# A Fourier mixer and a low-rank MLP on one core: first group of batch 0 closed by selection matmuls, loads held back, stage-2 loads issued at other steps

## The chip, the cores and the metric

The kernel runs on one core of a Trainium2 chip. The metric is the device time of one launch in microseconds (us). A core has a matrix engine (TensorE, PE in the profile; PEld are its weight loads), a vector engine (VectorE, DVE), a scalar engine (ScalarE, ACT), a general engine (GpSimd, POOL), and SyncE (SP), which here only issues transfers. Each engine works through its own list of instructions in order. DMAs are issued by SP, ACT and POOL, each in the order of its list; those that change the type on the way (f32 to f16) are issued by POOL. Matrix products end in PSUM (8 banks of 512 f32 a partition), and are brought to SBUF by ACT or DVE.

## The reference

For eight batches of 3136 tokens with 256 channels each, the reference filters along the tokens in the frequency domain, then applies a low-rank mixing along the tokens and a two-layer MLP along the channels, each with what it reads added:

```python
X = np.fft.rfft(x, axis=1)                                   # x: (8, 3136, 256)
y = np.fft.irfft(X * (filt_r + 1j * filt_i)[None], n=3136, axis=1)
u = y + (y.transpose(0, 2, 1) @ U @ V).transpose(0, 2, 1)    # U: (3136, 32), V: (32, 3136)
out = u + np.maximum(u @ w_ch1, 0.0) @ w_ch2                 # w_ch1: (256, 1024), w_ch2: (1024, 256)
```

## The kernel before

The transform of length 3136 is split as 64 x 49. For each batch there are four stages:

- Stage 1 (`st1`): the token axis of 64 points, by matmuls with the constant `wf`, for 49 residues in three tiles of 16 (`x[b, 0]` to `x[b, 2]`) and one last residue (`x[b, 3]`, tile `xl`). The result goes through DRAM (`ct1[b]`), since the next stage needs the residues on the partitions. `st1` is a generator of 13 pieces; each piece makes two matmuls of 256 columns and evicts one bank.
- Stage 2 (`two` in `plan_mid`, `stage2`): the residue axis, for eight "quads" of four frequencies; `load_a2` (`fetch`) brings one quad back from `ct1`. Then the product with the filter: `ta`, two halves of `tb`, and the sum `y` on POOL. The three products are made on DVE, or, for the quads in `on_pool`, on POOL after ACT has copied the bank (`pooled`). For this form the filter is rearranged in place into `fa` (= `fb`) and `fc`.
- Stage 3 (`three`, `stage3`, `out3`): back along the residues, two halves to a quad; ACT evicts to `esb`, SP stores a quad to DRAM (`ct2[b]`).
- Stage 4 (`stage4`): back along the 64 points, for groups of 512 tokens (`Group(b, c)`, c = 0 to 5; the last residues of two batches make one group of 128). `load_e2` fetches a group's tile `e` from `ct2` with the 64 frequency slots on partitions 0 to 63; `put_h` writes the low-rank part `h1` to partitions 64 to 95 of the same tile. So the matmul with `sv` adds the low-rank mixing as well. `low_rank` makes `h1` from all of `esb` and `uh`.

The MLP then runs over the groups. Each group has eight steps. A step makes two matmuls of the first layer (`mm1`, L488), one eviction with ReLU on ACT to the ring `hring` (L492), and one eighth of the second layer of the group before (`mm2_part`, L521, with the residual, L497). Steps 2 and 6 of a group also hold `stage4` of the next group. All other work of later batches is hung on steps by hand: `at(s, f, ...)` puts a call behind step s, `early[s]` ahead of it. There are 416 steps; `start[b]` is the first step of batch b; `later(s, n)` is n steps of full length after s.

Batch 0 is different, since nothing runs beside it. `turned` makes stage 1 with x as the stationary operand, and stores it in SBUF (`cm`, which lies in the space of `fc`); `mid_first` transposes it back on PE (`turn_a2`), and runs stage 2 and 3 with the filter as it was loaded: 16 halves `j`, a product `uv` with two results for each, and two matmuls with other constants in stage 3, so no sum is needed. For j = 7, 9, 12 and 14 POOL makes the product (L397), for the others DVE (L400). In `mid_first`, before these, POOL issues the loads of x of batch 1 and of the second weight `w2sb` (L384). After `mid_first` follow all of `st1(1)`, `low_rank(0)`, `put_h`, `stage4` of group 0, and the first half of `make_fa`; its second half is hung on steps 1 and 3. `keep_warm` are matmuls whose result is not used.

The plan of batch 1 begins five steps after the start of batch 0: stage 2 of its first quad at step 5, its last half of stage 3 at step 40, `load_e2(1, 0)` at step 41. Group 6, the first of batch 1, has its `stage4` on steps 46 and 47. For batch 2 stage 2 begins nine steps ahead of batch 1's first, and its first loads eight steps before that; stage 3 of batch 2 ends at 36 of the 50 steps of batch 1.

Of the kernel before, what the change touches and what calls it, by code (L numbers as in the profile page):

```python
# [14 lines left out]
SEQ = 3136  # L15
# [9 lines left out]
def _consts():  # L25
# [10 lines left out]
    wf = np.zeros((128, 25, 128))  # L36
    for h in range(2):
        wf[h::2, 0:24, 64 * h:64 * h + 64] = t1[:, 24 * h:24 * h + 24]
    wf[0:64, 24, 0:64] = t1[:, 48]
# [59 lines left out]
    return (wf.reshape(128, 25 * 128).astype(f16), w2.astype(f16), g3.astype(f16),  # L99
# [4 lines left out]
def kernel(  # L104
# [13 lines left out]
    names = ("wf", "w2", "g3", "s4", "su", "tw", "kr")  # L118
    wf_d, w2_d, g3_d, s4_d, su_d, tw_d, kr_d = (
# [22 lines left out]
    def bank(tag):  # L142
        of = {"m": (0, 1), "o": (2, 3), "w": (4,), "e": (7,), "f": (0, 1, 2, 3, 4, 7), "e0": (7, 4), "f0": (0, 1), "w1": (7, 5, 6)}[tag]
        turn[tag] = turn.get(tag, -1) + 1
        return psum[:, of[turn[tag] % len(of)], :]


    NH = 17
    hring = cst.tile([128, NH, 512], F16, name="hring")
# [3 lines left out]
    wf = cst.tile([128, 25, 128], F16, name="wf")  # L153
    for c in range(4):
        i = slice(8 * c, min(8 * c + 8, 25))
        nc.sync.dma_start(wf[:, i], wf_d.rearrange("p (i m) -> p i m", m=128)[:, i])
# [3 lines left out]
    def load_x(b, c, after=None):  # L160
        if c == 3:
            t = sb.tile([64, DM], F16, tag="xl", bufs=2, name="xl")
            nc.gpsimd.dma_start(t, dram(x.tensor, (b * SEQ + 48) * DM, [[NR * DM, 64], [1, DM]]))
        else:

            t = sb.tile([128, 4, XW], F16, tag="x", bufs=4, name="x")
            if after is not None:
                nc.gpsimd.tensor_copy(t[0:1, 0, 0:1], after[0:1, 0:1])
            for h in range(2):
                nc.gpsimd.dma_start(t[h:128:2, :, 0:2 * DM],  # L170
                                    dram(x.tensor, (b * SEQ + 24 * h + 8 * c) * DM,
                                         [[NR * DM, 64], [2 * DM, 4], [1, 2 * DM]]))
# [6 lines left out]
    def load_filters(a, z):  # L179
# [8 lines left out]
        if z == NK:  # L188
            for p0, src in ((0, filt_r), (64, filt_i)):
                nc.gpsimd.dma_start(fb[p0 + 25:p0 + NR, 31, :],  # L190
                                    dram(src.tensor, 32 * DM, [[64 * DM, 24], [1, DM]]))
            nc.gpsimd.dma_start(fb[0:25, 31, :], dram(filt_r.tensor, 0, [[64 * DM, 25], [1, DM]]))
            nc.gpsimd.dma_start(fb[65:89, 31, :],
                                dram(filt_i.tensor, 64 * DM, [[64 * DM, 24], [1, DM]]))
            nc.gpsimd.dma_start(fb[64:65, 31, :],
                                dram(filt_r.tensor, 1568 * DM, [[DM, 1], [1, DM]]))

    zero = cst.tile([128, 64], F16, name="zero")
    nc.vector.memset(zero, 0.0)
    nc.vector.memset(fb[96:128], 0.0)  # L200
    nc.scalar.copy(fb[32:64].rearrange("p s (k f) -> p (s k) f", f=64),
                   free(zero, 32, 64, 0, [[0, NK * DM // 64], [1, 64]]))
    nc.vector.memset(fc[:, 24:29, :], 0.0)
    usb = hflat[0:64, 0:NR * RANK]
    nc.gpsimd.dma_start(usb, moe_U.rearrange("(q r) p -> q (r p)", q=NQ))
# [4 lines left out]

# [7 lines left out]
    nc.scalar.dma_start(g3, g3_d.rearrange("p (f m) -> p f m", f=6))  # L218

# [3 lines left out]
    w2sb = cst.tile([128, 8, DM], F16, name="w2sb")  # L223
    vnat = hflat[64:96, 4704:4704 + SEQ]
    nc.gpsimd.dma_start(vnat, moe_V)
    nc.gpsimd.dma_start(w1sb, moe_w_ch1.rearrange("(h dd) c -> dd h c", h=2))

    sv = cst.tile([96, SEQ], F16, name="sv")
    kr = cst.tile([128, 96], F16, name="kr")

    def keep_warm(n):
        z = bank("f")
        for _ in range(n):
            nc.tensor.matmul(z, wf[:, 0, :], wf[:, 0:4, :].rearrange("p i m -> p (i m)"),
                             start=True, stop=True)
# [4 lines left out]
    def u_hat():  # L240
        ud = hflat[0:64, 1568:4704].rearrange("q (p c r) -> q p c r", c=2, r=NR)
        for p, eng in ((0, nc.vector.tensor_copy), (16, nc.scalar.copy)):
            eng(ud[:, p:p + 16], bass.AP(tensor=usb.tensor, offset=usb.offset + p,
                                         ap=[list(usb.ap[0]), [1, 16], [0, 2], [RANK, NR]]))
        for p in range(0, RANK, 8):
            z = bank("f")
# [4 lines left out]
            t = [sb.tile([98, NK, 8], F32, tag=tag, bufs=3, name="ut") for tag in ("ta", "tb")]  # L251
# [8 lines left out]
    def st1(b):  # L260
        for c in range(3):
            asb = sb.tile([128, 8, DM], F16, tag="asb", bufs=3, name="asb")
            for j in range(4):
                pf = bank("w" if b > 1 else "w1")
# [5 lines left out]
                if b == 1 and j % 2:  # L270
                    nc.vector.tensor_copy(dst, pf)  # L271
                else:
                    nc.scalar.copy(dst, pf)  # L273
                if j < 3:
                    yield
            for h in range(2):
                nc.sync.dma_start(dram(ct1[b], (16 * c + h) * 64 * DM,
                                       [[DM, 64], [128 * DM, 8], [1, DM]]), asb[64 * h:64 * h + 64])
            if 1 < b < NB - 1 and c:
                load_x(b + 1, c - 1)  # L280
            yield
        pf = bank("w" if b > 1 else "w1")
        nc.tensor.matmul(pf[0:64, 0:DM], wf[0:64, 24, 0:64], xt[b, 3], start=True, stop=True)
        al = sb.tile([64, DM], F16, tag="al", bufs=2, name="al")
        nc.scalar.copy(al, pf[0:64, 0:DM])
        nc.sync.dma_start(dram(ct1[b], 48 * 64 * DM, [[DM, 64], [1, DM]]), al)
        if 1 < b < NB - 1:
            load_x(b + 1, 2)
            load_x(b + 1, 3)
        yield  # L290


    cm = fc.rearrange("p s d -> p (s d)")

    def turned(c):
        for g in range(0, 8 if c < 3 else 1, 4):
            for hh in range(2):
                z = bank("f")
                n, o = 512, 3136 * hh + (8 * c + g) * 128
                if c < 3:  # L300
                    for i in range(4):
                        nc.tensor.matmul(z[:, 128 * i:128 * i + 128],
                                         xt[0, c][:, (g + i) // 2, DM * (i % 2) + 128 * hh:DM * (i % 2) + 128 * hh + 128],
                                         wf[:, 8 * c + g + i, :], start=(i == 0), stop=True,
                                         skip_group_check=True)
                else:
                    n = 64
                    nc.tensor.matmul(z[:, 0:n], xt[0, 3][:, 128 * hh:128 * hh + 128],
                                     wf[0:64, 24, 0:64], start=True, stop=True)
                if hh:  # L310
# [3 lines left out]


    esb = {}
# [6 lines left out]
    def out3(b, k, half, pe):  # L323
        if half == 0:
            esb[b, k] = sb.tile([98, 4, DM], F16, tag="esb", bufs=10, name="esb")
        nc.scalar.copy(esb[b, k][:, 2 * half:2 * half + 2, :].rearrange("p s d -> p (s d)"),  # L326
                       pe[0:98])
        if half:
            nc.sync.dma_start(dram(ct2[b], 4 * k * 98 * DM, [[DM, 98], [98 * DM, 4], [1, DM]]),
                              esb[b, k])  # L330

    def stage3(pe, parts, special):

        for n, (v, m, ms) in enumerate(parts):
            kw = dict(start=(n == 0), stop=(n == len(parts) - 1))
            if special:
                nc.tensor.matmul(pe[0:98, 0:DM], g3[:, m, :], v[:, 0:DM], skip_group_check=True, **kw)
        if special:
            for n, (v, m, ms) in enumerate(parts):
                nc.tensor.matmul(pe[0:98, DM:2 * DM], g3[:, ms, :], v[:, DM:2 * DM], start=False,  # L340
                                 stop=(n == len(parts) - 1), skip_group_check=True)
        else:
            for n, (v, m, ms) in enumerate(parts):
                nc.tensor.matmul(pe[0:98], g3[:, m, :], v, start=(n == 0), stop=(n == len(parts) - 1))  # L344
# [8 lines left out]

    def mid_first():
# [3 lines left out]
        def turn_a2(k):  # L358
            z = bank("f0").bitcast(F16)
            for i in range(4):  # L360
                for hh in range(2):
                    nc.tensor.transpose(z[:, DM * i + 128 * hh:DM * i + 128 * hh + 128],
                                        free(fc, 0, 128, 3136 * hh + 4 * k + i, [[32, 128]]), idn)
# [4 lines left out]
            if k in (1, 3):  # L368
                nc.vector.tensor_copy(a2[k], z[0:98])
            else:  # L370
                nc.scalar.copy(a2[k], z[0:98])

        todo = []

        def do3(j, uv):
            pe = bank("e0")
            stage3(pe, [(uv[:, 0], 2, 4), (uv[:, 1], 3, 5)], j == 15)
            out3(0, j // 2, j % 2, pe)

        for k in range(4):  # L380
            turn_a2(k)
        for c in range(4):
            load_x(1, c)
        nc.gpsimd.dma_start(w2sb, moe_w_ch2.rearrange("(cc t) e -> cc (t e)", t=8))  # L384
        for j in range(16):
# [6 lines left out]
            fin = free(fb, 0, 128, 2 * j * DM, [[0, 2], [1, 2 * DM]])  # L392
            if j in (7, 9, 12, 14):
                pc = sb.tile([128, 2, 2 * DM], F16, tag="pc", bufs=2, name="pc")
                nc.scalar.copy(pc, pz)
                uv = sb.tile([128, 2, 2 * DM], F16, tag="y", bufs=3, name="uv")
                nc.gpsimd.tensor_mul(uv, pc, fin)  # L397
            else:
                uv = sb.tile([128, 2, 2 * DM], F16, tag="ta", bufs=3, name="uv")
                nc.vector.tensor_mul(uv, pz, fin)  # L400
            if j < 4:
                turn_a2(j + 4)
            todo.append((j, uv))
            if len(todo) > 3:
                do3(*todo.pop(0))
        while todo:
            do3(*todo.pop(0))


    h1 = {}  # L410
# [10 lines left out]
    def low_rank_end(b):  # L421
# [4 lines left out]
        nc.scalar.copy(h1[b][64:96, :], pk[64:96, 0:DM])  # L426
# [5 lines left out]
    def load_e2(b, c):  # L432
# [5 lines left out]
        nc.sync.dma_start(t[0:64], dram(ct2[b], 8 * c * DM, [[NR * DM, 64], [1, n * DM]]))  # L438
# [19 lines left out]
    def stage4(gr, dh):  # L458
# [23 lines left out]
        nc.vector.tensor_copy(o, v)  # L482
# [17 lines left out]
    def mm2_part(gr, t):  # L500
        b = gr.b
        if gr.c == 6:
# [3 lines left out]
            nc.tensor.matmul(o, gr.h[t][:, 0:128], w2sb[:, t, :], start=(t == 0), stop=False,  # L506
# [261 lines left out]
```

## Time and profile before

| what | value |
|---|---|
| median of 5 runs | 557.65 us (557.52 to 560.01) |
| profiled execution, its own time | 557.52 us |
| its span, first to last instruction | 555.7 us |
| PE busy | 513.3 us (92%) |
| ACT busy | 390.6 us (70%) |
| DVE busy | 352.7 us (63%) |
| POOL busy | 282.4 us (51%) |
| moved by DMA | 92.06 MB, mean 166 GB/s |
| first matmul of the group loop (L488) | 61.48 us |

Times in the profile count from the first instruction of the span. An instruction group is named by line, engine, operation and what it writes and reads (`L488 PE MATMUL psum<-ut,w1sb`). "Idle before" is the time in which the engine stood still just before those instructions, with what ended it. The chain of waits goes back from the last instruction, at each step to what released it. A busy PE may still run at half clock; the row PEclk and a column of the stretches give the granted clock, 1.00 at full speed.

### The profile page before, as it was taken

The page shows a single profiled execution, that of the slowest core. Times are in us where ns is not written, and L with a number is a line of the kernel's source. Part 1 is how long each engine was busy: PE and PEld are TensorE (multiplying, and loading weights), DVE is VectorE, ACT ScalarE, POOL GpSimd, SP SyncE. Part 2 cuts the span into 40 slices and gives each one's busy share as a digit, 9 for nine tenths or more (in the row PEclk, how much of TensorE's full clock was granted, in tenths as well). Part 3 has the DMA queues.
Part 4 walks back from the last instruction along what each step waited for, and adds up shares of the span by engine and source line. Part 5 has one row for each costly group of instructions (what it writes and reads, how often), then busy time and mean ns, then how long its engine had stood idle before and what let it go on. Part 6 is the DMA issues. An engine that isn't in the chain of part 4 may idle for free.

```text
span 555.7 us, 11638 instructions
## 1 busy us (share of the span) xinstructions
PE 513.3 (92%) x4491; PEld 373.4 (67%) x4491; DVE 352.7 (63%) x409; ACT 390.6 (70%) x684; POOL 282.4 (51%) x194
## 2 busy tenths in 40 slices
PE   4867589996999999999999999999999999999996
PEld 2624356664767777677776777677786777777775
DVE  6754776755756686758746785858746887643332
ACT  8556868773787687767876788667777577765663
POOL 5778279951884065915683175806563297300000
PEclk8999999997999999999999999999999999999999
DMA  9997886894679468775879468765653554233212
GB/s 191 165 158 170 237 157 184 210 228 128 172 185 241 135 174 197 173 196 145 200 220 223 123 173 225 166 195 156 188 170 120 141 167 121 106 113 114 96 77 87
DMA packets 85432, 92.06 MB, mean 166 GB/s; under 512 B 6741, under 2 KB 69416, under 8 KB 85376
## 3 DMA queue, kind: packets, MB, share of 16 engines
q1 hardware_dynamic: 67968, 75.12, 45.7%
q0 software_dynamic: 16960, 15.91, 19.0%
q8 instruction: 35, 0.57, 0.4%
q10 hardware_dynamic: 448, 0.28, 0.2%
q14 instruction: 21, 0.17, 0.1%
HBM read 57.42 MB, written 49.77 MB: 193 GB/s over the span
## 4 chain that ended last, share of the span: by engine, by line
PE 70%; POOL 10%; DMA 7%; DVE 7%; ACT 4%; issue 2%; DVEq 0%; ACTq 0%; POOLq 0%; SPq 0%
PE psum L521 25%; PE psum L488 24%; PE psum L352 4%; PE psum L344 4%; PE psum L477 4%; PE psum L497 3%; PE psum L266 3%; POOL y L634 3%; DMA x<-in_x_dram 2%; POOL x L170 2%; DMA w1sb<-in_moe_w_ch_dram 2%; DVE ut L482 1%; DVE tb L632 1%; PE psum L416 1%; DMA ct<-esb 1%
## 5 line engine op out<-in xcount | busy, mean ns | idle before, releaser
L492 ACT ACTIVATE hring<-psum 128x512 f16<-128x512 f32 (+1 forms) x416 | 237.6, 576 | 103.3 <-PE psum L488 101.9
L488 PE MATMUL psum<-ut,w1sb 128*128 128x512 f16 (+1 forms) x832 | 240.2, 370 | 5.8 <-DVE ut L482 2.9
L521 PE MATMUL psum<-w2sb,hring 128*128 128x256 f16 x1536 | 231.0, 273 | 0.0
L634 POOL TENSOR_TENSOR y<-ta,tb 128x1024 f16<-128x1024 f16 x56 | 120.6, 2160 | 159.8 <-DVE tb L632 113.5
L521 PEld LDWEIGHTS <-hring 128*128 128x128 f16 x1536 | 143.2, 98 | 63.6 <-issue 3.5
L482 DVE CAST ut<-psum 128x512 f16<-128x512 f32 x96 | 71.0, 740 | 107.2 <-PE psum L477 87.2
L488 PEld LDWEIGHTS <-w1sb 128*128 128x128 f16 x832 | 104.7, 145 | 26.7 <-issue 9.9
L529 DVE COPY och<-psum 128x512 f32<-128x512 f32 x96 | 66.1, 688 | 47.3 <-PE psum L497 46.7
L326 ACT CAST esb<-psum 98x512 f16<-98x512 f32 x128 | 74.6, 586 | 24.1 <-PE psum L344 18.2
L628 DVE TENSOR_TENSOR ta<-psum,fb 128x1024 f16<-128x1024 f32 x41 | 49.9, 1217 | 7.9 <-PE psum L352 6.9
L273 ACT CAST asb<-psum 128x512 f16<-128x512 f32 x78 | 45.7, 589 | 12.3 <-PE psum L266 11.1
L497 PE MATMUL psum<-idn,ut 128*128 128x128 f16 x392 | 54.1, 220 | 0.0
L477 PEld LDWEIGHTS <-e 96*128 96x128 f16 x768 | 35.6, 98 | 25.6 <-issue 10.0
L630 DVE TENSOR_TENSOR tb<-psum,fc 64x1024 f16<-64x1024 f32 x41 | 50.3, 1226 | 0.9
L632 DVE TENSOR_TENSOR tb<-psum,fc 64x1024 f16<-64x1024 f32 x41 | 49.9, 1218 | 0.8
L477 PE MATMUL psum<-sv,e 96*128 96x64 f16 x768 | 38.6, 194 | 6.9 <-DMA e<-ct 4.1
L344 PE MATMUL psum<-y,g 128*98 128x512 f16 x105 | 39.9, 380 | 3.0 <-POOL y L634 1.6
L497 PEld LDWEIGHTS <-ut 128*128 128x128 f16 x392 | 38.4, 98 | 4.9
L628 POOL TENSOR_TENSOR ta<-pc,fb 128x1024 f16<-128x1024 f16 x15 | 32.4, 2157 | 10.5 <-ACT pc L638 10.5
L352 PE MATMUL psum<-a,w2t 98*128 98x512 f16 x113 | 34.3, 379 | 2.1 <-DVE tb L632 1.6
L266 PE MATMUL psum<-x,wf 128*128 128x256 f16 x168 | 31.3, 274 | 2.8 <-DVE asb L271 1.0
L630 POOL TENSOR_TENSOR tb<-pc,fc 64x1024 f16<-64x1024 f16 x15 | 31.9, 2125 | 1.2
(93 smaller groups left out, 367.8 us busy)
## 6 DMA issues: line engine op xcount, KB each, us to landing
out_dram<-och SPq DMA_DIRECT2D x47, 512.0 KB
ct<-esb SPq DMA_DIRECT2D x64, 196.0 KB
x<-in_x_dram POOLq DMA_DIRECT2D x48, 256.0 KB, 8.3
e<-ct SPq DMA_DIRECT2D x48, 256.0 KB
a<-ct SPq DMA_DIRECT2D x56, 196.0 KB
ct<-asb SPq DMA_DIRECT2D x42, 256.0 KB
wf<-wf SPq DMA_DIRECT2D x3, 256.0 KB
w1sb<-in_moe_w_ch_dram POOLq DMA_DIRECT2D x1, 512.0 KB, 8.4
```

The costliest lines, as they stand in the source:

```text
L326: nc.scalar.copy(esb[b, k][:, 2 * half:2 * half + 2, :].rearrange("p s d -> p (s d)"), pe[0:98])
L344: nc.tensor.matmul(pe[0:98], g3[:, m, :], v, start=(n == 0), stop=(n == len(parts) - 1))
L477: nc.tensor.matmul(pu[:, 64 * i:64 * i + 64], e2[b, c][:, i, 128 * dh:128 * dh + 128], sv[:, 64 * r:64 * r + 64], start=(i == 0), stop=Tru ...
L482: nc.vector.tensor_copy(o, v)
L488: nc.tensor.matmul(ph[:, 0:n], w1sb[:, dh, :, t], gr.ut[:, dh, 0:n], start=(dh == 0), stop=(dh == 1))
L492: nc.scalar.activation(h[:, 0:n], ph[:, 0:n], RELU)
L497: nc.tensor.matmul(o[:, dh * 128:dh * 128 + 128], gr.ut[:, dh, t0:t0 + n], idn, start=False, stop=(dh == 1), skip_group_check=True)
L521: nc.tensor.matmul(o, gr.h[tt][:, i * 128:(i + 1) * 128], w2sb[:, tt, :], start=(tt == 0), stop=False, skip_group_check=True)
L529: nc.vector.tensor_copy(gr.och[:, 2 * y:2 * y + 2, :].rearrange("p j d -> p (j d)"), gr.pc)
L628: eng.tensor_mul(ta, p, va)
L630: eng.tensor_mul(tb[0:64], p[64:128], vb[64:128])
L634: nc.gpsimd.tensor_add(ys[k], ta, tb)
```

## The change

It touches the prologue, batch 0, and the plans of batches 1 and 2.

- Constants: `wf` is stored once instead of twice side by side, and DVE doubles it with two masks (`pair`). `U` is loaded as f32 by SP instead of by a converting DMA of POOL. The loads of `sv` and `kr` come behind the first quad of stage 3, the rest of `sv` behind the last. New constants `sel` and `s4x` are loaded by ACT. `cm` gets a tile of its own. Zeroing of `fb` on ACT goes away; tiles use 113 partitions (`NZ`) instead of 128.
- Order of batch 0: `u_hat` is spread over the four `turned`. In `mid_first` the loads of x(1,0) and x(1,1) and the copy of `V` into `sv` stand on POOL ahead of the halves; two back-transposes instead of four come before the first half. POOL makes one product (j = 12) instead of four.
- Group 0: its tile `e` is loaded for slots 0 to 47 only, once quads 0 to 5 are stored. `pick` selects the other slots out of `esb` with `sel`, and a matmul with `s4x` adds them; a third pair of matmuls adds the low-rank part.
- Stage 1 of batch 1: three of its 13 pieces stay in `mid_first`, ten are hung on steps 0 to 7. The piece of x(1,3) comes before those of x(1,2). The stores of the third tile are issued by POOL.
- Held loads: POOL copies one element of `e2[0, 0]` into an added column of `w2sb`, and only then issues x(1,3), x(1,2) and `w2sb`.
- Filter: `make_fa` is cut into `make_fc` (eight copies on POOL), `make_neg` (DVE, steps 5 to 11) and `make_fa` (DVE at 12 and 13, POOL at 34 to 41), quad by quad.
- Plan of batch 1: quads 0, 1, 6 and 7 take the form with two products (`two_q`, `mul_q`, `three_q`), quads 3 and 5 are `pooled`, 2 and 4 on DVE. Stage 2 runs from step 15 to 37, stage 3 ends at step 40, `load_e2(1, 0)` is at step 40.
- Batch 2: its x is loaded at steps 13 to 16, behind the arrival of the first stage-2 load of batch 1; stage 1 begins at step 18 instead of 12, stage 2 four steps ahead of batch 1's first step instead of nine, the first three loads five steps ahead of that instead of eight; in each later step the load stands in front of stage 2. Quads 1, 3 and 5 are pooled instead of 2 and 5. Stage 3 ends at 39 of 50 steps. x of batch 3 is loaded at steps 40, 42, 44 and 45.

```diff
+    usb = hflat[0:64, 0:2 * NR * RANK].bitcast(F32)
+    nc.sync.dma_start(usb, moe_U.rearrange("(q r) p -> q (r p)", q=NQ))
+    wfc = hflat[:, 6272:6272 + 1604]
+    nc.sync.dma_start(wfc, wf_d)
...
+    for h in range(2):
+        nc.vector.tensor_scalar_mul(wf[:, :, 64 * h:64 * h + 64],
+                                    wfc[:, 0:1536].rearrange("p (i m) -> p i m", m=64),
+                                    wfc[:, 1600 + 2 * h:1602 + 2 * h].bitcast(F32))
...
+        def pick(j):
+            for i in range(2):
+                sl = 2 * (j - 12) + i
+                for g in range(4):
+                    nc.tensor.matmul(zp[32 * g:32 * g + 32], sel[:, g, 28 - 4 * sl:60 - 4 * sl],
+                                     esb[0, j // 2][:, 2 * (j % 2) + i, :], start=(sl == 0),
+                                     stop=(sl == 7), skip_group_check=True)
...
+            if ndone[0, k] == 2:
+                whole.append(k)
+                if k == 0:
+                    nc.sync.dma_start(sv[0:64, 0:512], s4_d[:, 0:512])
+                    nc.sync.dma_start(kr, kr_d)
+                if k == 5:
+                    load_e2(0, 0, 48)
+                if k == 6:
+                    load_e2(0, 1, 48)
+                if k == 7:
+                    load_e2(0, 1, 64, 48)
+                    nc.sync.dma_start(sv[0:64, 512:], s4_d[:, 512:])
+                    load_e2(0, 2)
+                    load_e2(0, 6)
...
-            if j in (7, 9, 12, 14):
+            if j == 12:
...
+        step1(1)
+        step1(1)
+        pick(14)
+        low_rank_part(7)
+        pick(15)
+        h1[0] = hp = sb.tile([128, DM], F16, tag="hp", bufs=1, name="hp")
+        nc.vector.tensor_copy(hp, ph)
+        zs = sb.tile([128, DM], F16, tag="zs", bufs=1, name="zs")
+        nc.scalar.copy(zs, zp)
+        keep_warm(2, psum[:, 7, :])
+        low_rank_end(0)
+        for dh in range(2):
+            for i in range(8):
+                nc.tensor.matmul(pu[dh][:, 64 * i:64 * i + 64],
+                                 e2[0, 0][0:48, i, 128 * dh:128 * dh + 128],
+                                 sv[0:48, 64 * i:64 * i + 64], start=(i == 0), stop=False,
+                                 skip_group_check=True)
+        for dh in range(2):
+            nc.tensor.matmul(pu[dh], zs[:, 128 * dh:128 * dh + 128], s4x, start=False, stop=False,
+                             skip_group_check=True)
+        step1(1)
+        for dh in range(2):
+            nc.tensor.matmul(pu[dh], h1[0][64:96, 128 * dh:128 * dh + 128], sv[64:96, 0:512],
+                             start=False, stop=True, skip_group_check=True)
...
     mid_first()
+    keep_warm(3, psum[:, 7, :])
+    nc.gpsimd.tensor_copy(w2sb[0:1, 0, DM:DM + 1], e2[0, 0][0:1, 0, 0:1])
+    load_x(1, 3)
+    load_x(1, 2)
+    nc.gpsimd.dma_start(w2sb[:, :, 0:DM], moe_w_ch2.rearrange("(cc t) e -> cc t e", t=8))
+    for k in (4, 0, 1, 6, 7):
+        make_fc(k, nc.gpsimd.tensor_copy)
+    put_h(0, 1)
...
+        def two_q(k, half):
+            box[k, half] = [psum[:, 5:7, :]]
+            for f in range(2):
+                stage2(psum[:, 5 + f], w2t[:, 128 * f:128 * f + 128],
+                       w2t[:, 256 + 128 * f:384 + 128 * f],
+                       a2[k][:, 2 * half * DM:2 * half * DM + 2 * DM], (k, half) == (7, 1))
...
+        if b == 1:
+            for k, q in ((0, 11), (3, 11), (1, 11), (5, 11), (2, 17), (4, 20), (6, 22), (7, 25)):
+                at(q, fetch, k)
+            for k, q, d in ((3, 17, 26), (5, 21, 31), (2, 23, 33), (4, 28, 37)):
+                at(q, two, k)
...
+            for k, qs in ((0, (15, 16)), (1, (19, 20)), (6, (33, 34)), (7, (36, 37))):
+                for half, q in enumerate(qs):
+                    at(q, two_q, k, half)
+                    early[q + 1].append((mul_q, (k, half)))
+                    at(q + (3 if k == 7 else 2), three_q, k, half)
+            return 40
-            at(later(s, -lead), fetch, k)
+            at(later(s, -5 if b == 2 else -9), fetch, k)
...
+    for n in (0, 0, 1, 1, 2, 3, 4, 5, 6, 7):
+        at(n, step1, 1)
+    at(13, lambda: load_x(2, 0, a2q[0][0:1, 0:1]))
+    for c in range(4):
+        if c:
+            at(13 + c, load_x, 2, c)
+        at((40, 42, 44, 45)[c], load_x, 3, c)
...
-            plan_st1(b, 12, (0, 1, 3, 4, 5, 7))
+            plan_st1(b, 18, (0, 3, 4, 5, 7))
...
-        m = later(start[b - 1], (5, -9, -12)[min(b, 3) - 1])
-        z = plan_mid(b, m, (2, 5) if b > 1 else (1, 3, 5))
+        m = later(start[b - 1], (16, -4, -12)[min(b, 3) - 1])
+        z = plan_mid(b, m, (2, 5) if b > 2 else (1, 3, 5))
```

## The prediction

> **What bounds the kernel now.** I read the slices of the span first (part 2 of the page), to see where TensorE (PE) is not full.
>
> ```profile
> PE   4867589996999999999999999999999999999996
> ...
> PEclk8999999997999999999999999999999999999999
> ```
>
> A slice is 13.9 us. From the tenth slice on PE is full; what it loses lies in the first ten, 0 to 140 us. So the steady part is bound by PE work and nothing in it can be won by moving transfers. Then I read the stretches of 4 us around the start of the group loop and around the step from batch 0 to batch 1 (columns: length, then busy us of PE, PEld, DVE, ACT, POOL, then the granted clock, DMA share, GB/s).
>
> ```profile
> 64.00:68.00 4.00, 2.11 (x17) 1.14 (x16) 3.61 (x6) 4.00 (x4) 0.90 (x3) 1.00 0.73 207
> 68.00:72.00 4.00, 2.03 (x15) 1.08 (x14) 3.60 (x8) 2.67 (x5) 4.00 (x6) 1.00 0.98 194
> ...
> 76.00:80.00 4.00, 4.00 (x30) 2.83 (x29) 2.42 (x3) 2.92 (x5) 4.00 (x2) 1.00 1.17 210
> ...
> 128.00:132.00 4.00, 1.25 (x13) 1.03 (x14) 0.56 (x1) 0.00 (x0) 0.00 (x0) 0.62 0.86 211
> 132.00:136.00 4.00, 3.57 (x21) 2.13 (x20) 3.88 (x6) 1.01 (x2) 0.00 (x0) 0.52 0.21 44
> ```
>
> PE is half idle at 64 to 72 while DVE and ACT are full, and starved at 128 to 132. Summed over all such stretches PE is busy 65.8 us between its first product of the loop (61.4, L488) and 140, so 12.8 us are idle there; from 140 to 540 it is idle under 5 us. The chain of waits then says what the prologue waited for, and who held the two worst places:
>
> ```profile
> 28.75 8.39 DMA w1sb<-in_moe_w_ch_dram
> ...
> 37.42 0.57 POOL w2sb L384
> 38.00 2.14 POOL uv L397
> ...
> 44.89 4.21 POOL uv L397 x2
> ...
> 120.05 6.78 DMA ct<-esb
> ...
> 126.97 3.65 DMA e<-ct
> ```
>
> At 28.75 POOL's DMA queue starts on w1sb; the instruction that issues the second weight waits 3.7 us for it (37.42), and the product uv stands behind it on POOL, so PE has a hole of 4.5 us before 40.18. The step to batch 1 is a round trip through memory: a store of 6.78 us and a load of 3.65 us.
>
> **What the Trainium skill says.** "TensorE: Matmul & The Clock Gate", Part 1: after an idle window of about 3.4 us PE runs at half clock until it has been busy as long. The trace agrees: after the wait of 4.1 us for e the clock is 0.62 and 0.52 in the two stretches above, about 2.5 us lost. "GPSIMD Engine Reference", Engine selection, has one-input operations on POOL at roughly line rate. The trace doesn't show that: its one such copy, L562, took 6946 ns for 3136 elements, 2.2 ns each. "SBUF — State Buffer", two separate sides: POOL and a DVE operation in a two-port mode exclude each other. The trace has L444 at 0.90 us while that POOL copy ran, its next two at 0.68 and 0.69: a delay, of the sort that the new POOL copies can bring. "DMA: Bandwidth & Descriptors", Anatomy of one DMA, puts about 2 us of fixed cost on a DMA; the round trips here are longer.
>
> **The change, part by part.**
>
> Loads before 20 us. The x of batch 0 is complete at 18.62 and its DMAs land one after another from 11.4, so transfers set this stretch. The constant wf goes from 800 to 401 KB, sv (392 KB) and kr (24) move behind stage 3, U becomes 392 KB instead of 196; sel (47) and s4x (128) come in: some 450 KB less in front of x. At the 200 GB/s of the last x DMAs (256 KB each 1.3 us, as POOL's waits for them show) that is 2.2 us. DVE gets the doubling of wf (two of 1536 elements, about 0.6 each by L544, 0.69 for 2048), three memsets and U's conversion; it is otherwise idle until x arrives near 11, so these cost nothing; if wf were later than x they would, up to 2 us.
>
> First half of the prologue. Stage 2 starts after two back-transposes instead of four, about 1 us sooner. The first product uv was at 24.52; I put it at 21.3.
>
> The uv products. 15 now run on DVE and one on POOL (4 before). DVE: 15 x 1.23 (L400, 1220 ns and the gap) + 0.7 for one a2 copy = 19.2, so the last ends near 40.7; before it was 47.8. Nothing waits for w2sb any more. ACT has in this time 16 x 0.59 (L326) + 6 x 1.01 (L371) + 1.02 = 16.5 of 19.2 us, so it follows.
>
> Group 0. Its load of e takes slots 0 to 47 alone, which quads 0 to 5 fill; half 11 is evicted near 39. Store and load: I take 6.5 (2.85 us for the last store of batch 0, from its issue at 51.2 to SP's next issue at 54.01, + 3.65), so e is there at 45.5. The bounds are 5 and 10.4 (6.78 + 3.65). The rest comes from esb by selection: 32 + 4 small matmuls, which lie beside this wait. After it: 16 matmuls of L477 (0.8), two of 512 columns (0.43), step1 (0.22), two more (0.43), an eviction of 0.74: first L488 at 48.1, and 46.5 to 52 by the bounds, against 61.4. Gain 13.3.
>
> What is carried into the loop. Ten of the 13 pieces of st1(1): 19 matmuls of 256 columns at 0.108 = 2.1 us of PE. Four quads of batch 1 take the form with two products, 4 matmuls more in stage 2 and 3 together: 4 x 4 x 0.215 = 3.4 us. Both are on the path, as PE is the bound: +5.5. Against them, per such quad, DVE does 2 x 1.22 instead of 3, with no POOL sum.
>
> First eight steps. Before, 61.4 to 72.3 with 4.3 us of PE work: 6.6 idle, since make_fa put 4 x (0.69 + 0.70) on DVE and 1.9 each on ACT. Now DVE has about 8.7 us (7 evictions 0.69, two 0.74, put_h, make_neg at half size) beside 6.1 us of PE: 2.9 idle. Gain 3.7. Small waits up to 120 (2.8) fall to about 1.0: gain 1.8.
>
> The held loads. POOL copies one element of e(0,0) into w2sb before it issues x(1,3), x(1,2) and the second weight. Behind this wait stand, in POOL's order, these three loads, five copies make_fc, the ct1 stores of c=2 and everything of batch 1. Released at 45.5, x(1,2) is issued by 47.5; beside it move sv's rest, e(0,1), e(0,2) and two ct1 stores, 2.7 MB with w2sb, 12.5 us at 220 GB/s. x(1,2) near 53 for step 4 at 53, w2sb near 58 for step 8 at 57.5: I charge 1 us; 0 if the queue is fair, 5 if w2sb takes 13.9 from issue as before.
>
> make_fc: five copies of 1024 elements, 0.9 (line rate of the skill at its 1.2 GHz, an estimate) to 2.2 us (L562) each, so POOL is free at 53 to 59, while step 7 wants to store ct1 at 56. Then store and a2 load, 6.5, before step 15 at 66.5. I charge 1 us (0 to 4). Eight halves of the new form share the banks 5 and 6, each with a product of 1.22 us between two stage-2 pairs of PE: 1 us (0 to 3).
>
> The step to batch 1. The last stage-3 half stays at step 40 and group 6 still needs e at step 46. The three a2 loads of batch 2 go to step 39, which is on SP just ahead of the last store, and x(3) to steps 40 to 45. I take 0 for this, and -6 to +4 as bounds: its 4.1 us wait and 2.5 us of slow clock can go, or grow. What is late next is the same load of e. Batch 2's stage 3 ends at 39 of 50 steps instead of 36, so its e must come within 6 steps, 7.3 us: +0.5 (0 to 4). Its third pooled quad and the 113 partitions for 128 change no path: POOL is under half busy there, and durations go by elements.
>
> Sum: -13.3 + 5.5 - 3.7 - 1.8 + 1 + 1 + 1 + 0.5 = -9.8. The profiled execution took 557.52 (span 555.7 and 1.8 around it), 0.13 below the median of 557.65, so 547.7; I say 547.5.
>
> **Rivals.** *All hidden* (540): the four charges fall away (-3.5), e is there at 44.5 (-1), and the step to batch 1 loses half of its 6.6 us (-3.3). For it: the DMA share falls to 0.06 at 80 to 84, so there is room; against it: the same round trip ends last. *Eaten by the step to batch 1* (555): the early a2 loads and x(3) hold the store, so 10.4 becomes 14 (+3.6), with 1 more of slow clock, and batch 2's step costs 3 instead of 0.5. For it: 291 GB/s when the store was slow; against it: 3 loads are only 588 KB. *The held POOL queue becomes the bound* (562, slower): the wait for e(0,0) delays everything behind it. If e lands at 49, the loop starts 3.5 us later; x(1,2), issued by 51 and 8.4 us on its way as the x of batch 2 was, comes at 59.4 and stops PE at step 4 for 3 us; w2sb with its 13.9 us costs 1.5 at step 8; two such holes bring 2.5 of slow clock; and what POOL then does late (x of batch 2, two pooled quads of 8.5 us) costs 3.5 more at the step to batch 1: +14. It decides against the change once e lands about 3 us later than I take, at these landing times. For it: 8.4 us to landing of x beside other traffic; against it: fewer loads are in flight.
>
> **How the numbers follow.** My forecast has 0.58 (own range 542 to 553), all hidden 0.22, eaten 0.07, held queue 0.13. From 537 to 556 leaves out the held queue and a twentieth below. A measurement tells 0.3%, 1.7 us, from no change: faster 0.83, same 0.04 (half of the eaten case), slower 0.13.
>
> **What would show it.** First L488-like product near 48 and no POOL wait on the first-layer weight before a product: right. uv on DVE without holes from 21 to 41. Waits of stage 1 on DMA x or of the second product on w2sb over 3 us: the held queue. A wait of PE on e at the step to batch 1 over 5 us: eaten. The prediction is wrong if the first product of the loop comes after 53, or if PE's idle time from there to the start of batch 1 is over 16 us or under 4.

## The result, and the profile after

The changed kernel takes 558.87 us (median of 43 runs, 555.86 to 562.28) against 557.18 us for the kernel before (80 runs, 552.70 to 561.83): a ratio of 1.0032 with the interval 1.0019 to 1.0045. It is slower by some 1.7 us, where 10 us of gain were forecast, and 558.87 lies above the range of 537 to 556.

The page of the changed kernel comes first: TensorE's busy time (part 1), then its slices and its clock (part 2).

```profile
PE 522.4 (94%) x4540; PEld 376.1 (67%) x4540; DVE 352.4 (63%) x413; ACT 375.7 (67%) x678; POOL 284.0 (51%) x205
...
PE   5896989977998999999999999999999999999996
...
PEclk9899799987999999999999999999999999999999
```

PE has 522.4 us of busy time instead of 513.3. The first three slices are fuller, as intended, but the clock now falls at two places after the start: in the fifth slice (56 to 70 us), and in the ninth and tenth (112 to 140 us); before it was in the tenth alone.

Where the lead went is seen by the start of the first product with the first-layer weight (L488 before, L610 after) of single steps, read from the two traces in us (step 415 is the last one):

| Step | 0 | 8 | 40 | 48 | 84 | 108 | 415 |
|---|---|---|---|---|---|---|---|
| Before | 61.48 | 70.32 | 118.15 | 135.34 | 176.22 | 205.21 | 549.62 |
| After | 47.42 | 61.72 | 111.50 | 133.50 | 173.72 | 207.11 | 551.83 |
| Lead | 14.06 | 8.60 | 6.65 | 1.84 | 2.50 | -1.90 | -2.21 |

The prologue wins 14.1 us, and four stretches spend them: 5.5 in steps 0 to 8, 1.9 in steps 8 to 40, 4.8 in steps 40 to 48, 4.4 in steps 84 to 108. From step 108 on next to nothing changes (0.3). The stretch from step 0 to step 52, before and after, in one row each (columns as in the prediction):

```profile
61.48:140.61 79.13, 66.11 (x545) 45.94 (x542) 52.10 (x63) 56.35 (x97) 50.08 (x35) 0.96 0.78 186
47.42:138.70 91.28, 75.33 (x571) 50.59 (x569) 50.22 (x68) 51.55 (x93) 46.46 (x43) 0.91 0.79 183
```

It is 12.15 us longer. PE is idle for 15.95 us of it instead of 13.02, so 2.9 are idle time, and 9.2 are busy time. In the stretches at half clock PE is busy 14.33 us instead of 4.65. Half of that difference, 4.8 us, is the slower clock (an estimate), and the other 4.4 are added work. The largest waits of PE in the loop (engine, what waits, for what; us in total, times, longest):

```profile
PE psum L599 <- DMA sv<-s: 4.7, 1, 4.7
PE psum L599 <- DMA e<-ct: 4.6, 1, 4.6
PE psum L399 <- DMA a<-ct: 3.8, 2, 2.5
```

The first is new, the second was 4.1 before (L477), the third is not among the eleven largest before (1.1 us and more). The stretches of 4 us around the first two show what follows each:

```profile
52.00:56.00 4.00, 0.00 (x0) 0.00 (x0) 0.00 (x0) 0.61 (x2) 1.66 (x3) 0.97 1.19 216
56.00:60.00 4.00, 3.35 (x24) 2.07 (x24) 2.22 (x4) 0.77 (x2) 0.00 (x0) 0.50 1.17 308
60.00:64.00 4.00, 4.00 (x25) 2.45 (x23) 3.88 (x10) 2.54 (x5) 0.72 (x1) 0.67 0.14 49
...
120.00:124.00 4.00, 3.57 (x14) 1.82 (x13) 1.23 (x1) 1.18 (x2) 0.00 (x0) 0.58 0.96 212
124.00:128.00 4.00, 0.32 (x2) 0.00 (x0) 0.00 (x0) 0.60 (x1) 0.00 (x0) 0.93 0.35 89
128.00:132.00 4.00, 3.08 (x25) 2.19 (x26) 2.35 (x3) 0.60 (x1) 0.00 (x0) 0.50 0.81 176
```

At 52 to 56 PE does nothing, with the DMA engines full (share 1.19). Then it runs at 0.50 and 0.67 of its clock. That agrees with the Trainium skill, "TensorE: Matmul & The Clock Gate", Part 1, which puts PE at half clock after an idle window of about 3.4 us: such a wait costs its own length and then a slow stretch. But a shorter wait can do the same here. The one of 2.50 us for a2, at 120.43 in the timeline below, is followed by the clock of 0.58 at 120 to 124. The timeline of the changed kernel (start, length, engine, line; in brackets the idle time before and what ended it) names the causes:

```profile
44.88 0.18 POOL L681 COPY w2sb<-e 1x1 f16<-1x1 f16 x1 [2.73 <-DMA e<-ct]
...
46.95 0.90 POOL L684 DMA_DIRECT2D w2sb<-in_moe_w_ch_dram  x1
47.28 0.45 SPq L470 DMA_DIRECT2D sv<-s  x1
...
47.90 5.27 POOL L405 COPY fc<-fb 49x1024 f16<-49x1024 f16 x5
...
56.65 0.59 PE L599 MATMUL psum<-sv,e 96*128 96x64 f16 x8 [4.67 <-DMA sv<-s]
...
112.00 2.45 POOL L187 DMA_DIRECT2D x<-in_x_dram  x4
113.80 1.37 SPq L362 DMA_DIRECT2D a<-ct  x3
115.22 0.43 SPq L376 DMA_DIRECT2D ct<-esb  x1
120.43 0.84 PE L399 MATMUL psum<-a,w2t 98*128 98x512 f16 x2 [2.50 <-DMA a<-ct]
125.19 0.49 SPq L559 DMA_DIRECT2D e<-ct  x1
128.92 0.58 PE L599 MATMUL psum<-sv,e 96*128 96x64 f16 x8 [4.59 <-DMA e<-ct]
```

The rest of `sv`, 328 KB issued at 47.28, is on its way for 9.4 us beside x(1,3), x(1,2), the second weight, the loads of `e` and the stores of `ct1`; all start within a few us of each other. The product that waits is `stage4` of group 1, which stands on steps 4 and 6 here and on 2 and 6 in the kernel before. At the step to batch 1 the last store of `esb` is issued at 115.22, behind three a2 loads in SP's queue and 0.8 us after POOL has issued four x of batch 3; its load follows only at 125.19. So the store takes 9.5 us from the end of its issue. In the kernel before it took 6.6 (120.36 to 126.97), with the last four x of batch 3 issued 8 us ahead of it (POOL, then SP):

```profile
109.49 2.54 POOL L170 DMA_DIRECT2D x<-in_x_dram  x4
...
120.05 0.31 SPq L329 DMA_DIRECT2D ct<-esb  x1
126.97 0.51 SPq L438 DMA_DIRECT2D e<-ct  x1
```

### The profile page after: what moved, and what is told of

Read it like the earlier page. It is cut to its first block, busy times and chain, and to the rows that moved or that the text cites. A ratio compares the mean times of both kernels' runs of the same rounds, so it can differ in the third digit from the quotient of the medians.

```text
span 558.0 us, 11737 instructions
## 1 busy us (share of the span) xinstructions
PE 522.4 (94%) x4540; PEld 376.1 (67%) x4540; DVE 352.4 (63%) x413; ACT 375.7 (67%) x678; POOL 284.0 (51%) x205
## 4 chain that ended last, share of the span: by engine, by line
PE 55%; POOL 5%; DVE 1%; ACT 1%; issue 1%; DMA 1%; ACTq 0%; POOLq 0%
PE psum L643 21%; PE psum L610 20%; PE psum L619 3%; PE psum L599 3%; PE psum L399 3%; PE psum L391 2%; PE psum L304 2%; POOL y L744 2%; POOL x L187 1%; PE psum L537 1%; POOL tb L742 1%; POOL ta L738 1%; POOL tb L740 1%; DMA a<-ct 1%; DVE ut L604 0%
## 5 line engine op out<-in xcount | busy, mean ns | idle before, releaser
L610 PE MATMUL psum<-ut,w1sb 128*128 128x512 f16 (+1 forms) x832 | 243.1, 374 | 1.2 <-DVE ut L604 0.7
L744 POOL TENSOR_TENSOR y<-ta,tb 113x1024 f16<-113x1024 f16 x52 | 112.5, 2168 | 157.2 <-DVE tb L742 120.7
L604 DVE CAST ut<-psum 128x512 f16<-128x512 f32 x94 | 69.5, 740 | 106.5 <-PE psum L599 93.3
L610 PEld LDWEIGHTS <-w1sb 128*128 128x128 f16 x832 | 105.2, 145 | 24.2 <-issue 6.0
L738 DVE TENSOR_TENSOR ta<-psum,fb 113x1024 f16<-113x1024 f32 x37 | 45.0, 1217 | 10.1 <-PE psum L399 6.7
L740 DVE TENSOR_TENSOR tb<-psum,fc 49x1024 f16<-49x1024 f32 x37 | 45.4, 1226 | 1.0
L742 DVE TENSOR_TENSOR tb<-psum,fc 49x1024 f16<-49x1024 f32 x37 | 45.1, 1218 | 1.0
L399 PE MATMUL psum<-a,w2t 98*128 98x512 f16 x120 | 36.9, 385 | 7.3 <-DMA a<-ct 3.8
L391 PE MATMUL psum<-y,g 113*98 113x512 f16 x98 | 37.4, 382 | 3.0 <-POOL y L744 1.6
L738 POOL TENSOR_TENSOR ta<-pc,fb 113x1024 f16<-113x1024 f16 x15 | 32.3, 2154 | 11.1 <-ACT pc L748 11.0
L304 PE MATMUL psum<-x,wf 128*128 128x256 f16 x168 | 33.2, 282 | 1.3 <-DVE ut L604 0.8
L740 POOL TENSOR_TENSOR tb<-pc,fc 49x1024 f16<-49x1024 f16 x15 | 31.8, 2120 | 1.2
```

The costliest lines, as they stand in the source:

```text
L399: nc.tensor.matmul(pz, w, a, start=True, stop=True)
L604: (nc.scalar.copy if gr is groups[0] and dh else nc.vector.tensor_copy)(o, v)
L610: nc.tensor.matmul(ph[:, 0:n], w1sb[:, dh, :, t], gr.ut[:, dh, 0:n], start=(dh == 0), stop=(dh == 1))
L738: eng.tensor_mul(ta, p[0:NZ], va)
L740: eng.tensor_mul(tb[0:NR], p[64:NZ], vb[64:NZ])
L744: nc.gpsimd.tensor_add(ys[k], ta, tb)
```

## The experiments

Each kernel starts from the changed one, and its diff is against that. Ratios are to the kernel before, from runs on the same chip; the changed kernel's is 1.0032. Single runs of one kernel spread by almost 1% to either side, so the intervals decide what may be claimed of times. Where they overlap, two profiles show where time went, not that a difference is sure. All of `sv` early, and x of batch 3 later, are tried alone and together first.

**1. The whole of `sv` behind quad 0**

```diff
-                    nc.sync.dma_start(sv[0:64, 0:512], s4_d[:, 0:512])
+                    nc.sync.dma_start(sv[0:64], s4_d)
...
-                    nc.sync.dma_start(sv[0:64, 512:], s4_d[:, 512:])
```

> Theory A (the rest of sv, loaded last of all, is a stall of its own): the 4.7 us wait of stage 4 of group 1 on sv goes, with the half clock after it (2.5 us); w2sb is late next, about 2 us. 552 to 556 us, 3 to 6 below the changed kernel. Rival B (all that is released at 45 us shares one full set of DMA engines, so any load moved away only uncovers the next): x(1,2) or w2sb takes over the whole wait, within 1.5 us of the changed kernel, 557 to 560.

Measured: 556.07 us, ratio 0.9997 (0.9969 to 1.0025), span 553.5 against 558.0. The time is at the upper end of theory A's range, and the interval just overlaps that of the changed kernel. The stretches of this kernel at the same place, same columns:

```profile
52.00:56.00 4.00, 4.00 (x36) 2.52 (x35) 3.09 (x6) 3.56 (x8) 2.72 (x4) 1.00 1.23 203
56.00:60.00 4.00, 2.92 (x29) 2.12 (x28) 3.88 (x9) 1.99 (x4) 1.15 (x1) 1.00 1.15 327
```

And two lines of its waits:

```profile
PE psum L399 <- DMA a<-ct: 5.5, 2, 3.5
PE psum L598 <- DMA e<-ct: 4.3, 1, 4.3
```

PE is full where it stood still, at full clock, although the DMA engines are as busy as before (1.23): it was the order of the loads, not their sum. Step 8 starts at 55.63, 6.1 us sooner than in the changed kernel; 1.7 of it are given back by step 16, where a2 loads are now waited for longer, and 4.5 reach the end of the profile. The wait for `e` at the step to batch 1 stays.

**2. x of batch 3 eight steps later**

```diff
-        at((40, 42, 44, 45)[c], load_x, 3, c)
+        at((48, 50, 52, 53)[c], load_x, 3, c)
...
-            plan_st1(b, later(start[b - 1], -54 if b == 3 else -60), (0, 3, 4, 7) if b == 3 else (0, 4, 7))
+            plan_st1(b, later(start[b - 1], -44 if b == 3 else -60), (0, 1, 3, 4, 5, 7) if b == 3 else (0, 4, 7))
```

> x of batch 3 at steps 48 to 53 instead of 40 to 45, its stage 1 from step 55 on. Theory A (x of batch 3 fills the DMA engines while the last store of batch 1's stage 3 and batch 2's first stage-2 loads are on their way): the store falls from 9.5 us to 5 or less, the waits of PE on a (2.5) and on e (4.6) fall to under 3 in sum and the slow clock after them goes: 550 to 554 us. Rival B (the store waits behind the three stage-2 loads of batch 2 on SP and their own traffic): waits change by under 2 us, 556 to 560.

Measured: 559.13 us, ratio 1.0038 (1.0012 to 1.0064). Its timeline has the same store and load of `e` on SP:

```profile
115.30 1.21 SPq L362 DMA_DIRECT2D a<-ct  x3
116.56 0.40 SPq L376 DMA_DIRECT2D ct<-esb  x1
120.10 0.49 SPq L559 DMA_DIRECT2D e<-ct  x1
```

Its waits:

```profile
PE psum L304 <- DMA x<-in_x_dram: 4.4, 2, 3.2
...
PE psum L599 <- DMA e<-ct: 2.3, 1, 2.3
```

The store falls from 9.5 to 3.1 us, still behind three a2 loads on SP: the x loads of POOL made it long. So of theory A the store came true, and the time (550 to 554) did not. Step 52 starts at 131.92, 6.8 us ahead of the changed kernel, but by step 72 all of that is lost, to a new wait for x itself.

**3. Both**

> Both edits. If the two losses are independent, the gains add: 545 to 551 us, clearly below the kernel before. If the lead of batch 0 is always lost again at the step to batch 1, no faster than the second edit alone.

Measured: 555.14 us, ratio 0.9968 (0.9944 to 0.9991), span 553.1. That is below the changed kernel's interval, but not the 545 to 551 that two added gains would give. Step 52 starts at 127.06, 13.5 us ahead of the kernel before, and step 72 at 160.26, as in experiment 1 (160.37). The timeline points to the reason (POOL, then PE):

```profile
126.72 1.30 POOL L187 DMA_DIRECT2D x<-in_x_dram  x2
...
134.62 2.12 POOL L743 TENSOR_TENSOR y<-ta,tb 113x1024 f16<-113x1024 f16 x1
136.68 2.52 POOL L187 DMA_DIRECT2D x<-in_x_dram  x4
...
142.39 0.38 PE L304 MATMUL psum<-x,wf 128*128 128x256 f16 x2 [2.33 <-DMA x<-in_x_dram]
```

POOL was idle from 108.7 to 124.7, but two loads stand behind a sum that waits for DVE, and the other five behind four operations of a pooled quad of 2.1 us each. So the time given back is put down to POOL's order, and not to a loss that a faster start brings with it; experiment 5 tests that.

**4. No held loads**

```diff
-    nc.gpsimd.tensor_copy(w2sb[0:1, 0, DM:DM + 1], e2[0, 0][0:1, 0, 0:1])
```

> The one copy on POOL that holds x(1,3), x(1,2) and the second weight for e(0,0) is left out. POOL waited 2.7 us there, so they are issued 2.7 us sooner. If the hold protects e(0,0): e(0,0) lands 1 to 3 us later and the loop starts later by as much, w2sb sooner: 557 to 561 us. If the hold is the loss: 554 to 556.

Measured: 559.1 us, ratio 1.0047 (1.0023 to 1.0072), which overlaps the changed kernel's interval. The first product is at 47.67 instead of 47.42. The wait for `sv` falls to 2.7 us, those for a2 and `e` become 5.7 and 5.3. The hold neither wins nor loses what can be measured, and the first product was not later without it; it moves the wait.

**5. x of batch 3 held for the arrival of `e`.** In addition to experiment 1, all four x are issued at step 44, behind a POOL copy of one element of `e2[1, 0]` into the first of them, so ahead of the pooled quad and behind the round trip.

```diff
-        at((40, 42, 44, 45)[c], load_x, 3, c)
+        at(44, lambda c=c: load_x(3, c, None if c else e2[1, 0][0:1, 0, 0:1]))
...
-            plan_st1(b, later(start[b - 1], -54 if b == 3 else -60), (0, 3, 4, 7) if b == 3 else (0, 4, 7))
+            plan_st1(b, later(start[b - 1], -46 if b == 3 else -60), (0, 3, 4, 5, 7) if b == 3 else (0, 4, 7))
```

> sv early as in the first run; x of batch 3 is issued by POOL at step 44, but behind a copy of one element of e(1,0), so all seven loads start as soon as that tile is there, while POOL is idle; stage 1 of batch 3 from step 52. Theory A (the store and the load of e at the step to batch 1 lost to x of batch 3, and moving x to steps 48 to 53 only shifted the loss because POOL came to it late, at 127 and 137 us, behind products): the lead at step 52 stays to step 72, waits on x under 1 us: 548 to 552 us. Rival B (the lead is lost to the later start of batch 2's plan whatever the transfers do): as with both edits before, 554 to 557.

Measured: 550.88 us, ratio 0.9899 (0.9867 to 0.9931), span 550.0. The timeline has all x of batch 3 in one place:

```profile
120.48 3.81 POOL L187 DMA_DIRECT2D x<-in_x_dram  x6 [0.32 <-POOL x L185]
```

Step 52 starts at 128.68 and step 72 at 157.09, 3.2 us ahead of experiment 3, although its prologue happened to be 1.6 us later in this profile (49.80 against 48.23). The interval lies below those of experiments 1 and 3: the traffic of x(3) at the step to batch 1, and POOL's order when it is moved, are shown as causes. Whether issuing at step 44 without the hold would do as well was not tried.

**6. The store ahead of the a2 loads too.** In addition to experiment 5, the first a2 loads of batch 2 come one step later, behind the store, and so do the load of `e` and what follows it.

```diff
-            at(later(s, -5 if b == 2 else -9), fetch, k)
+            at(later(s, -4 if b == 2 else -9), fetch, k)
...
-        plan_rest(b, z)
+        plan_rest(b, later(z, 1) if b == 1 else z)
```

> The run with held x of batch 3, and the last store of batch 1's stage 3 goes ahead of the three stage-2 loads of batch 2 on SP, the load of e(1,0) behind them. If SP's order costs the store its 1.2 us, the remaining wait on e (2.4 us) falls to about 1.2: 1 us below the held run. If the loads' traffic then meets the store, or a comes late, no gain or 1 us worse.

Measured: 548.26 us (546.69 to 553.64), ratio 0.9864 (0.9823 to 0.9905), span 546.3. SP in its timeline:

```profile
109.27 0.32 SPq L376 DMA_DIRECT2D ct<-esb  x1
109.76 1.27 SPq L362 DMA_DIRECT2D a<-ct  x3
111.86 0.49 SPq L558 DMA_DIRECT2D e<-ct  x1
```

Its waits on DMA:

```profile
PE psum L642 <- DMA w2sb<-in_moe_w_ch_dram: 1.8, 1, 1.8
...
PE psum L598 <- DMA e<-ct: 1.3, 1, 1.3
```

The store takes 2.3 us, PE waits 1.3 us for `e`, and 1.8 once for the second weight (at step 8), and steps 40 to 48 take 11.56 us, against 22.00 in the changed kernel and 17.19 before. The step over experiment 5 is 3.7 us in the profile, of which 2.4 were there at step 0 already; in the times the two intervals overlap, so the gain from the order on SP alone is not sure. This version beats both kernels: it is 1.4% under the one before.

**7. One product of two left out.** Experiment 5, with one of the two products in stages 2 and 3 of quads 0, 1, 6 and 7 of batch 1 left out: 16 matmuls of 512 columns of the computation are missing; DVE's product keeps its size.

```diff
-            for f in range(2):
+            for f in range(1):
...
-            stage3(pe, [(uv[:, 0], 2, 4), (uv[:, 1], 3, 5)], (k, half) == (7, 1))
+            stage3(pe, [(uv[:, 0], 2, 4)], (k, half) == (7, 1))
```

> The run with held x of batch 3, and quads 0, 1, 6 and 7 of batch 1 make only one of their two stage-2 products and one of their two stage-3 products (16 matmuls of 512 columns left out, the DVE product keeps its size), so what is computed for these quads is not the filter. If the second products are on PE's path as I counted, 3.4 us below the held run, 545 to 549 us; if they lie in PE's idle time, within 1 us of it.

Measured: 550.89 us, ratio 0.9912 (0.9884 to 0.9941), as experiment 5. Steps 16 to 46 become shorter, 45.01 us for 47.24, but steps 46 to 48 longer, 7.99 for 6.61, with this in its waits, where experiment 5 had one of 2.8:

```profile
PE psum L598 <- DMA e<-ct: 4.8, 2, 3.8
```

Most of what PE saves ahead of the round trip it waits for at the round trip.

**8. Batch 2 sooner.** Experiment 5, with stage 1 of batch 2 done by step 35, its first a2 loads two steps and its stage 2 three steps sooner; stage 3 ends at 34 of the 50 steps instead of 39.

```diff
-            plan_st1(b, 18, (0, 3, 4, 5, 7))
+            plan_st1(b, 18, (0, 1, 3, 4, 5, 7))
...
-            at(later(s, -5 if b == 2 else -9), fetch, k)
+            at(later(s, -4 if b == 2 else -9), fetch, k)
...
-        m = later(start[b - 1], (16, -4, -12)[min(b, 3) - 1])
+        m = later(start[b - 1], (16, -7, -12)[min(b, 3) - 1])
```

> The run with held x of batch 3; stage 1 of batch 2 uses six of eight steps, is done at step 35 instead of 37, its first stage-2 loads are at step 37 (ahead of the last store by three steps) and its stage 2 begins at step 41 instead of 44, so its stage 3 ends at 34 of 50 steps instead of 39. Theory A (between steps 84 and 108 the changed kernel needs 4.4 us more than the kernel before, because batch 2's plan is five steps later: two quads' work is done there, and quads 6 and 7 are squeezed): 2 to 4 us of it come back, 546 to 549 us. Rival B (that stretch is long because of three pooled quads): no gain there, 550 to 552.

Measured: 548.41 us, ratio 0.985 (0.9799 to 0.9901), an interval that overlaps experiment 5's. Its profiled execution has a wait of 6.0 us near step 49 that no other run shows, so only one stretch of it is read: steps 84 to 108 take 30.51 us, against 33.38 in experiment 5, 33.39 in the changed kernel and 28.99 before.

**9. Two pooled quads in batch 2.** Experiment 8, with quads 2 and 5 of batch 2 pooled instead of 1, 3 and 5, as before the change.

```diff
-        z = plan_mid(b, m, (2, 5) if b > 2 else (1, 3, 5))
+        z = plan_mid(b, m, (2, 5) if b > 1 else (1, 3, 5))
```

> As the run with batch 2 sooner, and two pooled quads in batch 2 (2 and 5) as in the kernel before, instead of three. Theory A: within 1 us of it. Rival B: 2 us or more below it, and the stretch of steps 84 to 108 shorter by as much.

Measured: 548.92 us, ratio 0.9857 (0.9804 to 0.9909), span 547.1; steps 84 to 108 take 30.50 us. The third pooled quad costs nothing there; of the 4.4 us of that stretch the later plan accounts for 2.9. For the other 1.5 the trace of experiment 9 has one wait of PE in this stretch, 1.67 us for a sum `y` on POOL (at 169.67), where the kernel before has 0.2 us of waits. Not all of the 2.9 are a gain: part of batch 2's work moves to earlier steps, and from step 0 to 108 experiment 9's profile is only 0.8 us shorter than experiment 5's (148.46 against 149.24). Experiments 6 and 8 together were not tried.

## Why the prediction was wrong

**Right: the prologue.** The first product is at 47.42 for the forecast 48.1. The products uv run on DVE from 21.38 to 40.56 (forecast 21.3 to 40.7; 21.3 and the 19.2 of its sum make 40.5), and the hold is released at 44.88 (forecast 45.5).

**Right: the held queue isn't the bound.** That rival (562) gave a time nearer to the measured one than the forecast did, but by luck: another cause made the time long. POOL waits 2.7 us at the hold, the five `fc` copies take 1.05 us each, and leaving the hold out changes nothing in the time (experiment 4). No wait for x of batch 1 over 3 us came up.

**Wrong: "First eight steps ... Gain 3.7".** The stretch took 14.30 us for 8.84 before, a loss of 5.5 where this term, the pieces of stage 1 (+2.1) and "The held loads ... I charge 1 us" together gave -0.6. The step named `sv`'s rest among the 2.7 MB in flight and priced the arrival of x(1,2) and `w2sb` only. It is `sv` that came last, at 56.65, and PE stood 4.67 us and then ran at half clock. Experiment 1 takes that out and keeps 4.5 us in its profile. Its steps 0 to 8 take 7.1 us, 1.7 less than before, where the gain of 3.7 and the added 2.1 made 1.6: but for `sv` the term came true. That is in part luck: its "6.6 idle" reaches to 72.3, past step 8 (70.32), and counts 4.3 us of PE work where the trace has 5.9 busy; in the eight steps themselves PE was idle 3.4 us. And 8.7 us of DVE beside 6.1 of PE leave 2.6, not 2.9.

**Wrong: "The step to batch 1 ... I take 0".** It lost 4.8 us. The argument against the rival "eaten by the step to batch 1", "3 loads are only 588 KB", counted the a2 loads and left out the 1 MB of x(3) (four of 256 KB, at 112.00) that POOL issues just before. The Trainium skill, "DMA: Bandwidth & Descriptors", Issuing engines are not separate DMA queues, says that DMAs of all issuers share the 16 engines; here x on POOL's queue took a store on SP's queue from 3.1 to 9.5 us (experiment 2). That rival's mechanism held, and its store was priced well enough: it had 14 us for store and load, measured are 13.3 (115.65 to 128.92). Experiments 5 and 6 undo it. Its own sign, a wait for `e` over 5 us, was not reached (4.6).

**Too small: "+0.5" for batch 2's later plan.** Steps 84 to 108 cost 4.4 us. In them PE is busy 30.27 us for 28.51 before, since work of batch 2 that was done earlier now lies there, and idle 3.12 us for 0.48. "Its e must come within 6 steps" looked at the last transfer alone. 2.9 us of the stretch come back when the plan starts three steps sooner and ends five sooner (experiments 8 and 9), but part of that is work moved again.

**Right in size: "+3.4" for four quads with two products, and "Small waits ... gain 1.8".** In steps 8 to 40 PE is busy 46.46 us for 42.72 before, 3.7 more, and idle 3.3 us for 5.1:

```profile
70.32:118.15 47.83, 42.72 (x348) 30.42 (x347) 31.07 (x36) 35.72 (x64) 41.97 (x27) 1.00 0.83 185
61.72:111.50 49.78, 46.46 (x362) 32.10 (x361) 33.12 (x44) 34.38 (x62) 33.73 (x28) 0.99 0.77 183
```

Still, leaving the 16 added matmuls out wins nothing that can be seen (experiment 7): the round trip behind them sets the end while it ends last.

So the sum failed in terms that it put at or near nothing. A lead of 14 us was real, and it lay ahead of two places that are bound by transfers. The change moved more transfers to both, and the two stretches around them took 10.3 us; the rest went to added work and the later plan. The prediction's limits for being wrong did not show this: the first product came well before 53, and PE's idle time from there to batch 1 was 15.95 us, just under the 16 named. They left out the time that PE is busy at half clock.

## What to carry to other kernels

When loads are released together, price the arrival of every one of them against its first use, in queue order, not only of those that the change is about. A lead won ahead of a round trip through memory is kept only if the round trip starts earlier and stays as short: hold bulk loads of other queues behind the arrival of what the critical store brings (experiment 5), and try that store first in its queue (experiment 6, where only the profile shows the gain). When moving such a load, check what stands in front of it on the engine that issues it.

## What the runs showed of the hardware

- One store of 196 KB took 9.5, 6.6, 3.1 and 2.3 us from the end of its issue to the load that waits for it, by what was in flight beside it and ahead of it. For a DMA that POOL issues the Trainium skill ("DMA: Bandwidth & Descriptors", Anatomy of one DMA) gives a fixed part of about 2 us and one by size. For 196 KB that makes 2.5 us, an estimate; it fits only the shortest of these stores, which SP issues.
- A POOL copy of 49 x 1024 f16 took 1.05 us (five in 5.27), 1.0 ns for each element of a partition; the strided copy L562 of the kernel before took 2.2 ns for each. The two also differ in partitions (49 and 32), so that the stride is the reason is not shown. The price of such a copy has to be taken from a row with the same access.
- PE fell to half clock after waits shorter than the 3.4 us named above: after one of 2.50 us in the changed kernel (0.50 from 120.64 to 124.05), and in experiment 6 after one of 1.78 us at 57.88, with 0.91 idle shortly before it (0.50 from 58.42 to 61.83).
